# Clustered attention and its feed-forward: x split in PSUM and turned by one transposing DMA per pair of heads, and three PSUM banks handed out by a stored list

## The chip, the cores and the metric

One Trainium2 chip, one core of it. The metric is the time of one execution on the device in microseconds (us), lower is better; the time given is the median of several runs.

## The reference

```python
def _attn_ref(q, k, v, centroids):            # 4 x 8 x 768 x 64, 16 centroids of each head
    ...                                       # q_assign, k_assign: nearest centroid by cosine
    mask = q_assign[:, :, :, None] == k_assign[:, :, None, :]
    scores = scale * np.matmul(q, k.transpose(0, 1, 3, 2))
    scores = np.where(mask, scores, -1000000000.0)
    ...                                       # softmax over the keys
    return np.matmul(attn, v).astype(np.float32)

def _moe_ref(x, w_in, w_out):                 # 3072 x 512, 512 x 2048, 2048 x 512
    h = x @ w_in
    g = np.where(h >= 1, h, np.where(h <= -1, 0.0, (h + 1) ** 2 / 4.0))
    return (g @ w_out).astype(np.float32)
```

The attention's output, with the eight heads side by side, is the x of the second function.

## The kernel before

The work is cut into 12 units: a unit is one batch (of 4) and 256 of its 768 queries. A unit has four pairs of heads. For each pair, `at_scores` multiplies q by k on TensorE four times (two heads, two blocks of 128 queries), `soften` and `at_soft` take the exponential on VectorE and ScalarE and split it into two float16 parts (ScalarE the high part, GpSimd the low one, tile `hl` or `word`), and a transposing DMA on SyncE's queue (SP) turns both parts into `pT`, a ring of three buffers. `at_av` (L1178) multiplies `pT` by v into half of PSUM bank `banka`.

What `at_av` then does for units 1 to 11 is what the change touches. VectorE multiplies the result by the reciprocal row sums into the SBUF tile `rb` (`xn`, L1194 to L1199). TensorE turns `rb` back into the same place of `banka` in two float32 transpositions against the identity `idf` (L1202 to L1207). ScalarE copies it to float16, `x` high, and VectorE subtracts for `x` low (L1208 to L1210). That happens 44 times: 11 units of four pairs. Unit 0 has a path of its own (`at_av_first`) that is left alone.

`ffn1` (L1341) multiplies the weights by a unit's x, all four pairs in one accumulation, 24 matmuls of 256 columns for each of 8 blocks of the hidden layer; `ffn2` (L1373) multiplies the result `g` by the second weights into `pair` bank 83. Both run some units behind the attention, mixed into it. The weights are read, rounded and split on VectorE and ScalarE during the first units.

PSUM: two double banks `pair`, `banka`, and three banks `bankh`, `banki`, `bankj` that a `Ring` (L459) hands out in turn to `ffn1`, to the labels of the clusters and to small sums.

The order of the instructions is set by a planner. Every operation is recorded as a node with a price (L129); `Recorder.issue` (L349) simulates the engines forward and backward `BASE` times, moves the priorities by 141 stored seeds (`NUDGES`, L50), simulates once more, and each engine gets its instructions in that order. An engine works strictly in its order, SP too: a DMA that waits for its data holds up all DMAs behind it.

Of the kernel before, what the change touches and what calls it, by code (L numbers as in the profile page):

```python
# [10 lines left out]
F16 = mybir.dt.float16  # L11
BF16 = mybir.dt.bfloat16
F32 = mybir.dt.float32
U32 = mybir.dt.uint32
AF = mybir.ActivationFunctionType
ALU = mybir.AluOpType
# [29 lines left out]
TURN, TURN_WAIT = dict(vector=185, gpsimd=118), 200  # L46

LOOK, MARGIN = 0.4, 4000
BASE = 11
NUDGES = (  # L50
# [16 lines left out]
)  # L67


# [11 lines left out]
class Recorder:  # L81
# [9 lines left out]
    def __init__(self, tc):  # L91
        self.tc, self.nc = tc, tc.nc
        self.leads = []
        self.nodes, self.seen, self.open, self.step, self.ev = [], {}, None, -99, 0
        for name in ("tensor", "scalar", "vector", "gpsimd", "sync"):
            setattr(self, name, Engine(self, name, getattr(tc.nc, name)))
# [362 lines left out]
class Ring:  # L459


    def __init__(self, bufs):
        self.bufs, self.i = bufs, -1

    def extend(self, buf):

        n = (self.i + 1) % len(self.bufs)
        self.bufs, self.i = [buf] + self.bufs[n:] + self.bufs[:n], -1

    def __call__(self, *shape, dtype):  # L470
        self.i += 1
        return view(self.bufs[self.i % len(self.bufs)], shape, dtype)


def view(buf, shape, dtype):
    n = 1
    for k in shape:
        n *= k
    ap = buf.bitcast(dtype)[:, :n]
    if len(shape) > 1:  # L480
        names = "abcd"[: len(shape)]
        ap = ap.rearrange(
            "p (" + " ".join(names) + ") -> p " + " ".join(names), **dict(zip(names[1:], shape[1:]))
        )
    return ap
# [3 lines left out]
def tile_clustered_attention_moe(  # L489
# [11 lines left out]
    B, H, S, D = q.shape  # L501
# [5 lines left out]
    P = 128  # L507
    T = S // P
    NP = H // 2
    CT = 2  # L510
    NCH = T // CT
    CQ = CT * P
# [16 lines left out]
    rec = Recorder(tc)  # L529
    const = ctx.enter_context(tc.tile_pool(name="const", bufs=1))  # L530
    psum = ctx.enter_context(tc.tile_pool(name="psum", bufs=1, space=PSUM))
    rings = {}

    def tiles(name, n, size):
        return [const.tile([P, size // 4], U32, name=f"{name}{i}") for i in range(n)]

    def new(tag, shape, dtype, n=1):

        if tag not in rings:
            size = mybir.dt.size(dtype)  # L540
            for k in shape:
                size *= k
            rings[tag] = Ring(tiles(tag, n, -(-size // 32) * 32))
        return rings[tag](*shape, dtype=dtype)


    slots = tiles("kv", NP, 3 * 3072)

    qs = tiles("q", 2, 8192)
    rings["qn"] = Ring(tiles("qn", 1, 4096))  # L550
    rings["o"] = Ring(tiles("o", 1, 4096))
    rings["vb"] = rings["o"]

# [4 lines left out]
    halves = wk[1:] + blocks[:-1]  # L558
    rings["w32"] = Ring(wk[:1])
    rings["x"] = Ring(tiles("x", 3, 4096))  # L560
    rings["g"] = Ring(tiles("g", 2, 2048))

    nb = tiles("n", 1, 2 * 3072)[0]
    nats = [nb[:, :768], nb[:, 768:]]
    x1, x2 = rings["x"].bufs[1:3]
    k_one = [view(x[:, i * 384 : (i + 1) * 384], [T, 2, D], BF16) for x in (x2, x1) for i in range(2)]
    rings["hl"] = Ring(tiles("hl", 3, 3072))
    rings["koT"] = Ring([x[:, i * 384 : (i + 1) * 384] for x in (rings["o"].bufs[0], rings["hl"].bufs[2]) for i in range(2)])
    q_one, q_oneT = (view(x[:, :512], [NP * CT, P], BF16) for x in rings["hl"].bufs[:2])
    q_one = q_one.rearrange("p n (j c) -> p n j c", j=2)  # L570
# [4 lines left out]

    pair = [psum.tile([P, 1024], F32, name=f"pair{i}") for i in range(2)]
    bank_a, *one = [psum.tile([P, 512], F32, name=f"bank{x}") for x in "ahij"]
    hid = Ring(one)
    av = Ring([bank_a[:, :CQ], bank_a[:, CQ:]])
    start = cycle([0, 1]).__next__  # L580

    def early():
# [595 lines left out]
    def at_av(b, hp, c):  # L1178
        u = b * NCH + c
        if u == 0:  # L1180
            return at_av_first(hp)
        e, kv = A.pop((b, hp, c)), KV[b, hp]
        pv = px = av(CQ, dtype=F32)
        for t in range(CT):
            with rec.group():
                for j in range(2):
                    to = pv[:, (t * 2 + j) * D : (t * 2 + j + 1) * D]
                    for kc in range(T):
                        for i, (va, pa) in enumerate(((0, 0), (1, 0), (0, 1))):
                            rec.tensor.matmul(  # L1190
                                to, e["pT", t][:, pa * T + kc, j], kv["vs"][:, va, j, kc * D : (kc + 1) * D],
                                start=(kc == i == 0), stop=(kc == T - 1 and i == 2),
                            )
        xn = new("rb", [CT * 2, D], F32)  # L1194
        rr = e["rs"].rearrange("p (j t) -> p t j", j=2).unsqueeze(3).to_broadcast([P, CT, 2, D])
        rec.vector.tensor_tensor(
            out=xn.rearrange("p (t j) d -> p t j d", j=2), in0=pv.rearrange("p (t j d) -> p t j d", t=CT, j=2),
            in1=rr, op=ALU.mult,
        )  # L1199
        if hp == 0:  # L1200
            X[u] = new("x", [2, NP, CQ], F16)
        with rec.group():  # L1202
            for t in range(CT):
                rec.tensor.matmul(
                    px[:, t * P : (t + 1) * P], xn[:, 2 * t : 2 * t + 2].rearrange("p j d -> p (j d)"), idf,
                    start=True, stop=True, is_transpose=True,
                )  # L1207
        hi, lo = X[u][:, 0, hp], X[u][:, 1, hp]  # L1208
        rec.scalar.copy(hi, px)
        rec.vector.tensor_tensor(out=lo, in0=px, in1=hi, op=ALU.subtract)  # L1210

    X = {}

# [127 lines left out]
    def ffn1(u, f):  # L1341
        if u == 0:
            return ffn1_first(f)
        if u == 2 and f == 0:
            more = dict(r=wk[0][:, :512], g=wk[0][:, 512:], sS=word[:, :768], hl=word[:, 768:1536], qn=blocks[-1])
            for name, buf in more.items():
                rings[name].extend(buf)
        e = FS[u, f]
        x = X[u]
        ph = hid(2, CQ, dtype=F32)  # L1350
        for s in range(2):
            with rec.group():
                for hp in range(NP):
                    for i, (wa, xa) in enumerate(((0, 0), (0, 1), (1, 0))):
                        rec.tensor.matmul(
                            ph[:, s],
                            w1[f][:, wa, hp, s * P : (s + 1) * P],
                            x[:, xa, hp],
                            start=(hp == 0 and i == 0),
                            stop=(hp == NP - 1 and i == 2),  # L1360
                        )
        phf = ph.rearrange("p s q -> p (s q)")

        r = new("hl" if u == NU - 1 else "r", [2 * CQ], F32, 1)
        rec.vector.tensor_scalar(out=r, in0=phf, scalar1=e["lo"], scalar2=e["hi"], op0=ALU.max, op1=ALU.min)
        rec.scalar.activation(out=r, in_=r, func=AF.Square, bias=e["ra"], scale=e["rs"])
        rec.vector.scalar_tensor_tensor(out=r, in0=phf, scalar=e["gs"], in1=r, op0=ALU.mult, op1=ALU.max)
        g = new("g", [2, 2 * CQ], F16)
        rec.scalar.copy(g[:, 0], r)
        rec.gpsimd.tensor_tensor(out=g[:, 1], in0=r, in1=g[:, 0], op=ALU.subtract)  # L1370
        F[u, f] = g
# [184 lines left out]
```

## Time and profile before

| | |
|---|---|
| median of 3 runs | 839.02 us (838.34 to 839.78) |
| the profiled execution | 836.59 us |
| its span, first to last instruction | 834.8 us |
| TensorE busy | 819.3 us, 98% |
| VectorE, ScalarE, GpSimd busy | 631.6, 646.8, 485.1 us |
| DMA queue of SP, share of 16 engines | 83.5% |

The profiled execution lies 2.4 us below the median of the runs, and 1.8 us of it lie outside the span. A busy TensorE counts the modelled end of each matmul, so the true cost of an instruction is read from start to start. All instructions pass through one helper, so every row carries the line L363, and groups are told apart by tile names.

### The profile page before, as it was taken

How to read it: one execution, taken by the hardware profiler on the slowest of the kernel's cores; microseconds unless marked ns; L12 is line 12 of the kernel's file. 1: busy time of each engine (PE TensorE's matmuls, PEld its weight loads, DVE VectorE, ACT ScalarE, POOL GpSimd, SP SyncE). 2: the span in 40 equal slices, each digit the busy share in tenths (PEclk: the TensorE clock that was granted, in tenths of full speed). 3: DMA queues.
4: the chain of work that ended last, by engine and by line, in shares of the span. 5: the costliest groups of instructions: out<-in, count | busy, mean ns of one | idle time of the engine just before them, and what ended most of it. 6: DMA issues, size and time to landing. Idle time of an engine off the chain costs nothing.

```text
span 834.8 us, 21762 instructions
## 1 busy us (share of the span) xinstructions
PE 819.3 (98%) x8495; PEld 586.2 (70%) x8495; DVE 631.6 (76%) x1430; ACT 646.8 (77%) x1168; POOL 485.1 (58%) x541
## 2 busy tenths in 40 slices
PE   9998999999999999999999999999999999999998
PEld 7655767667667676777677677677767777676776
DVE  4999999999997767578888767579987776554322
ACT  5999976889878788787788788788887697766322
POOL 2004756568767667656767676656666666665121
PEclk9999999999999999999999999999999999999999
DMA  9869999998999979999999988999999869665100
GB/s 332 271 169 165 179 225 226 224 181 158 206 181 163 195 167 182 174 184 175 173 197 164 198 171 157 178 192 199 178 185 162 163 137 162 106 130 95 20 26 26
DMA packets 405415, 141.44 MB, mean 169 GB/s; under 512 B 373952, under 2 KB 397504, under 8 KB 405312
## 3 DMA queue, kind: packets, MB, share of 16 engines
q1 hardware_dynamic: 405312, 140.05, 83.5%
q8 instruction: 66, 1.08, 0.5%
q14 instruction: 37, 0.30, 0.1%
HBM read 40.40 MB, written 6.29 MB: 56 GB/s over the span
## 4 chain that ended last, share of the span: by engine, by line
PE 76%; DVE 14%; DMA 4%; issue 3%; ACT 2%; POOL 1%; SPq 0%; DVEq 0%; POOLq 0%
PE pair L363 37%; PE banka L363 11%; PE banki L363 10%; PE bankh L363 9%; PE bankj L363 9%; DVE sS L363 4%; DVE w L363 3%; DMA q<-in_q_dram 1%; DMA w<-in_moe_w_out_dram 1%; DVE r L363 1%; DVE n L363 1%; DVE wk L363 1%; POOL hl L363 1%; DMA pT<-hl 1%; DMA kv<-n 1%
## 5 line engine op out<-in xcount | busy, mean ns | idle before, releaser
L363 POOL TENSOR_TENSOR hl<-sS,hl 128x384 f16<-128x384 f32 x212 | 210.0, 1011 | 96.1 <-ACT hl L363 70.1
L363 PE MATMUL pair<-w,g 128*128 128x512 f16 (+2 forms) x796 | 202.6, 393 | 0.0
L363 PEld LDWEIGHTS <-w 128*128 128x128 f16 x1848 | 178.0, 98 | 30.5 <-issue 1.3
L363 DVE CUSTOM_DVE_ANT_0 sS<-pair,zero,er 128x768 f32<-128x768 f32 x157 | 158.8, 1012 | 48.2 <-PE pair L363 39.5
L363 ACT ACTIVATE sS<-sS,sbi 128x768 f32<-128x768 f32 x157 | 146.5, 933 | 53.9 <-DVE sbi L363 50.0
L363 PE MATMUL pair<-kv,q 128*128 128x384 f16 (+1 forms) x768 | 158.3, 341 | 2.1 <-DVE sbi L363 1.9
L363 PEld LDWEIGHTS <-g 128*128 128x128 f16 x762 | 73.0, 98 | 68.6
L363 PEld LDWEIGHTS <-pT 128*128 128x128 f16 x3168 | 103.0, 98 | 9.4 <-issue 0.6
L363 PEld LDWEIGHTS <-q 128*128 128x128 f16 x880 | 71.6, 97 | 48.3 <-issue 8.0
L363 PE MATMUL banka<-kv,pT 128*128 128x64 f16 x3168 | 105.4, 193 | 0.0
L363 ACT CAST hl<-sS 128x768 f16<-128x768 f32 x106 | 87.4, 825 | 1.7 <-DMA pT<-hl 0.7
L363 PE MATMUL banki<-x,w 128*128 128x256 f16 (+1 forms) x672 | 86.0, 280 | 0.0
L363 PE MATMUL bankh<-x,w 128*128 128x256 f16 (+1 forms) x672 | 85.8, 280 | 0.1
L363 PEld LDWEIGHTS <-wk 128*128 128x128 f16 x606 | 58.0, 98 | 34.8 <-issue 0.6
L363 POOL TENSOR_TENSOR hl<-word,hl 128x384 f16<-128x384 f32 x70 | 63.1, 921 | 31.3 <-ACT hl L363 20.4
L363 PE MATMUL bankj<-x,w 128*128 128x256 f16 (+1 forms) x632 | 80.5, 278 | 0.3 <-DVE r L363 0.3
L363 POOL TENSOR_TENSOR word<-sS,word 128x384 f16<-128x384 f32 x70 | 64.0, 932 | 24.8 <-ACT word L363 22.6
L363 PE MATMUL pair<-w,wk 128*128 128x512 f16 x324 | 76.3, 373 | 0.0
L363 POOL TENSOR_TENSOR g<-r,g 128x512 f16<-128x512 f32 x32 | 39.8, 1244 | 26.1 <-ACT g L363 26.1
L363 ACT ACTIVATE word<-word,sbi 128x768 f32<-128x768 f32 x35 | 32.7, 935 | 20.3 <-DVE sbi L363 19.8
L363 DVE CUSTOM_DVE_ANT_0 word<-pair,zero,er 128x768 f32<-128x768 f32 x35 | 35.5, 1015 | 13.5 <-PE pair L363 12.8
L363 ACT ACTIVATE r<-r,f_ra,f_rs 128x512 f32<-128x512 f32 x44 | 35.6, 809 | 13.0 <-DVE r L363 12.9
(294 smaller groups left out, 1319.3 us busy)
## 6 DMA issues: line engine op xcount, KB each, us to landing
w<-in_moe_w_out_dram SPq DMA_DIRECT2D x14, 512.0 KB, 4.4
kv<-in_k_dram SPq DMA_DIRECT2D x16, 384.0 KB, 4.5
q<-in_q_dram SPq DMA_DIRECT2D x12, 512.0 KB, 5.3
kv<-in_v_dram SPq DMA_DIRECT2D x16, 384.0 KB, 4.0
out_dram<-o SPq DMA_DIRECT2D x11, 512.0 KB, 3.8
w<-in_moe_w_in_dram SPq DMA_DIRECT2D x10, 512.0 KB, 7.8
word<-in_moe_w_in_dram SPq DMA_DIRECT2D x6, 512.0 KB, 5.5
o<-in_v_dram SPq DMA_DIRECT2D x8, 384.0 KB, 4.0
```

Source lines behind the costliest of these rows:

```text
L363: fn(*args, **kw)
```

## The change

The product is scaled in place in PSUM by VectorE. ScalarE then copies it to float16 into the first half of a `rb` of the same size (1 KB a partition), VectorE writes the remainder into the second half, and one transposing DMA on SP turns the four blocks of 128x128 (high and low of the two query blocks) into `x`, which is now laid out by pair, then high and low. The TensorE transpositions are gone. A `Ring` can take its places from a stored string; `bankh`, `banki`, `bankj` are handed out by such a string of 214 digits, the other rings go on in turn. `BASE` is 2 instead of 11, and the seeds are 129 other ones.

```diff
-BASE = 11
+PICKS = {'hid': '0000101220110012000122112212112101202201120212020110...'}
+BASE = 2
...
     def __call__(self, *shape, dtype):
-        self.i += 1
-        return view(self.bufs[self.i % len(self.bufs)], shape, dtype)
+        self.i = int(next(self.picks, (self.i + 1) % len(self.bufs)))
+        return view(self.bufs[self.i], shape, dtype)
...
-    hid = Ring(one)
+    hid = Ring(one, "hid")
...
-        xn = new("rb", [CT * 2, D], F32)
         rr = e["rs"].rearrange("p (j t) -> p t j", j=2).unsqueeze(3).to_broadcast([P, CT, 2, D])
-        rec.vector.tensor_tensor(
-            out=xn.rearrange("p (t j) d -> p t j d", j=2), in0=pv.rearrange("p (t j d) -> p t j d", t=CT, j=2),
-            in1=rr, op=ALU.mult,
-        )
+        pf = pv.rearrange("p (t j d) -> p t j d", t=CT, j=2)
+        rec.vector.tensor_tensor(out=pf, in0=pf, in1=rr, op=ALU.mult)
+        xn = new("rb", [2, CQ], F16)
+        rec.scalar.copy(xn[:, 0], pv)
+        rec.vector.tensor_tensor(out=xn[:, 1], in0=pv, in1=xn[:, 0], op=ALU.subtract)
         if hp == 0:
-            X[u] = new("x", [2, NP, CQ], F16)
-        with rec.group():
-            for t in range(CT):
-                rec.tensor.matmul(
-                    px[:, t * P : (t + 1) * P], xn[:, 2 * t : 2 * t + 2].rearrange("p j d -> p (j d)"), idf,
-                    start=True, stop=True, is_transpose=True,
-                )
-        hi, lo = X[u][:, 0, hp], X[u][:, 1, hp]
-        rec.scalar.copy(hi, px)
-        rec.vector.tensor_tensor(out=lo, in0=px, in1=hi, op=ALU.subtract)
+            X[u] = new("x", [NP, 2, CQ], F16)
+        rec.sync.dma_start_transpose(
+            out=X[u][:, hp].rearrange("p a (t q) -> p (a t) q", q=P), in_=xn.rearrange("p a f -> p (a f)")
+        )
...
-                            x[:, xa, hp],
+                            x[:, hp, xa],
```

The order of every engine changes with the seeds. Two places matter below. The first is SP's end: `pT` is the turned exponential, `rb` the split product, `x_75` the x of unit 11. Before:

```order
L363 DMA_TRANSPOSE pT_146<-hl_81 128x12x128
L363 DMA out_dram<-o_68 128x1024
L363 DMA_TRANSPOSE pT_147<-hl_79 128x12x128
L363 DMA_TRANSPOSE pT_147<-hl_80 128x12x128
L363 DMA_TRANSPOSE pT_145<-word_71 128x12x128
L363 DMA_TRANSPOSE pT_145<-hl_81 128x12x128
L363 DMA_TRANSPOSE pT_146<-hl_79 128x12x128
L363 DMA_TRANSPOSE pT_146<-hl_80 128x12x128
L363 DMA_TRANSPOSE pT_147<-word_71 128x12x128
L363 DMA_TRANSPOSE pT_147<-hl_81 128x12x128
L363 DMA out_dram<-o_68 128x1024
L363 DMA out_dram<-o_68 128x512 x2
```

And with the change:

```order
L363 DMA_TRANSPOSE pT_147<-hl_80 128x12x128
L363 DMA_TRANSPOSE pT_145<-hl_81 128x12x128
L363 DMA_TRANSPOSE x_75<-rb_159 128x4x128
L363 DMA_TRANSPOSE pT_145<-word_71 128x12x128
L363 DMA_TRANSPOSE pT_146<-hl_79 128x12x128
L363 DMA_TRANSPOSE pT_146<-hl_80 128x12x128
L363 DMA_TRANSPOSE pT_147<-hl_81 128x12x128
L363 DMA_TRANSPOSE x_75<-rb_159 128x4x128
L363 DMA_TRANSPOSE pT_147<-word_71 128x12x128
L363 DMA_TRANSPOSE x_75<-rb_159 128x4x128
L363 DMA out_dram<-o_68 128x1024
L363 DMA out_dram<-o_68 128x512 x2
```

One transposition of x stands among every four of `pT`, with others behind it, and the last one stands after the last `pT`.

The second place is TensorE from the last product with v (`banka<-kv_64`) to the first use of unit 11's x. Before, with the first row of each run of equal ones:

```order
L363 MATMUL banka<-kv_64,pT_147 128x64
...
L363 MATMUL banki<-x_74,w_72 128x256
...
L363 MATMUL pair_83<-w_72,wk_69 128x512
...
L363 MATMUL banka<-idf,rb_159 128x128 x2
...
L363 MATMUL banki<-x_74,w_72 128x256
...
L363 MATMUL pair_83<-w_72,g_76 128x512
...
L363 MATMUL bankj<-x_75,wk_70 128x256
```

And with the change:

```order
L363 MATMUL banka<-kv_64,pT_147 128x64
...
L363 MATMUL pair_83<-w_72,wk_69 128x512
...
L363 MATMUL bankh<-x_74,w_72 128x256
...
L363 MATMUL pair_83<-w_72,g_76 128x512
...
L363 MATMUL banki<-x_75,wk_70 128x256
```

The runs between them are 12 of 256 columns, 12 of 512, the transpositions, 12 of 256 and 12 of 512 before, and 6 of 512, 12 of 256 and 12 of 512 now.

## Rows read from the trace of the kernel before

**Rows 1.** The page: busy time of each engine, the granted clock of TensorE in 40 slices, and the chain that ended last, by engine.
```profile
PE 819.3 (98%) x8495; PEld 586.2 (70%) x8495; DVE 631.6 (76%) x1430; ACT 646.8 (77%) x1168; POOL 485.1 (58%) x541
PEclk9999999999999999999999999999999999999999
PE 76%; DVE 14%; DMA 4%; issue 3%; ACT 2%; POOL 1%; SPq 0%; DVEq 0%; POOLq 0%
```

**Rows 2.** Busy time of each engine by stretch: start and end of the stretch, its length, then busy us (instructions) of PE, PEld, DVE, ACT and POOL, the granted clock, the DMA share and GB/s.
```profile
0.00:160.00 160.00, 149.12 (x1302) 105.77 (x1303) 146.17 (x309) 134.49 (x245) 63.69 (x93) 1.00 0.90 224
160.00:782.00 622.00, 621.18 (x6819) 443.81 (x6819) 470.07 (x1100) 496.85 (x901) 411.06 (x440) 1.00 0.89 168
782.00:835.00 53.00, 48.96 (x377) 36.64 (x374) 15.31 (x21) 15.47 (x23) 10.39 (x9) 1.00 0.06 21
...
0.00:40.00 40.00, 36.73 (x350) 27.96 (x351) 27.50 (x73) 30.23 (x51) 6.21 (x35) 1.00 0.88 304
40.00:100.00 60.00, 54.09 (x475) 37.82 (x474) 59.38 (x135) 57.76 (x117) 23.34 (x27) 1.00 0.81 169
100.00:160.00 60.00, 58.30 (x484) 40.00 (x481) 59.29 (x106) 46.50 (x79) 34.13 (x32) 1.00 1.00 226
160.00:220.00 60.00, 59.86 (x625) 40.96 (x625) 58.09 (x137) 54.16 (x94) 41.45 (x38) 1.00 0.90 183
400.00:460.00 60.00, 59.75 (x673) 42.59 (x672) 51.64 (x131) 50.19 (x90) 42.66 (x48) 1.00 0.99 174
```

**Rows 3.** Waits of TensorE from 160 us to the end (its matmuls, then its weight loads), in full but for two groups of issue: engine, what it was about to do, what it waited for, us in total, times, longest.
```profile
PE bankj L363 <- DVE r L363: 0.3, 1, 0.3
PE bankj L363 <- DMA kv<-n: 0.3, 1, 0.3
...
PEld L363 <- DMA kv<-n: 0.6, 2, 0.4
PEld L363 <- DVE n L363: 0.6, 1, 0.6
PEld banka L363 <- DVE rb L363: 0.5, 2, 0.3
```

**Rows 4.** The same for its matmuls in the first 160 us, two rows of nine.
```profile
PE banki L363 <- ACT pT L363: 1.6, 3, 0.7
PE bankj L363 <- ACT pT L363: 1.5, 3, 1.0
```

**Rows 5.** The timeline around one end of a pair: start, us, engine, what.
```profile
408.05 0.81 PE L363 MATMUL pair<-kv,q 128*128 128x384 f16 x4
408.19 0.42 DVE L363 TENSOR_TENSOR rb<-banka,rs 128x256 f32<-128x256 f32 x1
...
408.70 0.40 PE L363 MATMUL banka<-idf,rb 128*128 128x128 f32 x2
...
408.94 1.47 PE L363 MATMUL bankj<-x,w 128*128 128x256 f16 x12
```

**Rows 6.** Groups of equal instructions over the whole span: busy us, mean ns of one, idle before.
```profile
L363 DVE TENSOR_TENSOR rb<-banka,rs 128x256 f32<-128x256 f32 x44 | 18.5, 420 | 11.8 <-PE banka L363 11.4 <-PE bankj L363 0.2
L363 DVE TENSOR_TENSOR x<-banka,x 128x256 f16<-128x256 f32 x44 | 18.2, 416 | 9.3 <-ACT x L363 9.2
L363 PE MATMUL banka<-idf,rb 128*128 128x128 f32 x88 | 17.1, 276 | 1.0 <-DVE w_am L363 1.0
L363 ACT CAST x<-banka 128x256 f16<-128x256 f32 x44 | 15.8, 361 | 7.5 <-PE banka L363 7.3
L363 DVE TENSOR_TENSOR bankj<-bankj,mx 128x256 f32<-128x256 f32 x6 | 2.6, 428 | 0.1
```

**Rows 7.** Busy time of the instructions that touch `rb` alone, by stretch, columns as in rows 2 without POOL.
```profile
100.00:160.00 60.00, 1.58 (x8) 0.96 (x8) 1.64 (x4) 0.00 (x0) 1.00 1.00 226
160.00:220.00 60.00, 1.18 (x6) 0.77 (x6) 1.25 (x3) 0.00 (x0) 1.00 0.90 183
```

**Rows 8.** SP's issue of the one transposition of four 128x128 blocks (`q` of one pair) that starts at 407.0 us, with the ns for which it held SP and its time from issue to landing, then the longest wait of SP over the whole span.
```profile
L363 SPq DMA_TRANSPOSE q<-w x1: 1189/1189/1189, 407.0 to 407.0; - x1
DMA to landing us min/median/max: 2.4/2.4/2.4
...
SPq L363 <- POOL hl L363: 130.8, 76, 4.1
```

**Rows 9.** All transposing DMAs of `pT<-hl` and `q<-w`: count, median us to landing.
```profile
pT<-hl SPq DMA_TRANSPOSE x141, 4.1
q<-w SPq DMA_TRANSPOSE x11, 4.4
```

**Rows 10.** The end of the attention, from the chain that ended last (start, us, what) and from the timeline.
```profile
776.45 2.10 PE banka L363 x72
778.55 1.31 PE banki L363 x12
779.86 2.59 PE pair L363 x12
...
778.92 0.41 DVE L363 TENSOR_TENSOR rb<-banka,rs 128x256 f32<-128x256 f32 x1
...
782.28 0.38 PE L363 MATMUL banka<-idf,rb 128*128 128x128 f32 x2
...
782.50 1.47 PE L363 MATMUL banki<-x,w 128*128 128x256 f16 x12
782.70 0.37 ACT L363 CAST x<-banka 128x256 f16<-128x256 f32 x1 [2.97 <-PE banka L363]
783.11 0.42 DVE L363 TENSOR_TENSOR x<-banka,x 128x256 f16<-128x256 f32 x1 [3.77 <-ACT x L363]
```

More of the change, by code (lines that the diff above doesn't have):

```diff
@@ L48 @@
 LOOK, MARGIN = 0.4, 4000
-BASE = 11
+PICKS = {'hid': '0000101220110012000122112212112101202201120212020110210021201101200022110220010012100112202211210120112022200201100221221010011222001101122120210001211111122111202001212211000221121100002012221011111111111010101010'}
+BASE = 2
 NUDGES = (
[16 rows of a table removed]
[15 rows of a table added]
 )
@@ L459, with __init__ @@
 class Ring:
-    def __init__(self, bufs):
-        self.bufs, self.i = bufs, -1
+    def __init__(self, bufs, name=None):
+        self.bufs, self.i, self.picks = bufs, -1, iter(PICKS.get(name, ""))
     def extend(self, buf):
-        n = (self.i + 1) % len(self.bufs)
-        self.bufs, self.i = [buf] + self.bufs[n:] + self.bufs[:n], -1
+        self.bufs = self.bufs + [buf]
     def __call__(self, *shape, dtype):
-        self.i += 1
-        return view(self.bufs[self.i % len(self.bufs)], shape, dtype)
+        self.i = int(next(self.picks, (self.i + 1) % len(self.bufs)))
+        return view(self.bufs[self.i], shape, dtype)
 def view(buf, shape, dtype):
@@ L542, in new @@
                 size *= k
-            rings[tag] = Ring(tiles(tag, n, -(-size // 32) * 32))
+            rings[tag] = Ring(tiles(tag, n, -(-size // 32) * 32), tag)
         return rings[tag](*shape, dtype=dtype)
@@ L549, in tile_clustered_attention_moe @@
     qs = tiles("q", 2, 8192)
-    rings["qn"] = Ring(tiles("qn", 1, 4096))
+    rings["qn"] = Ring(tiles("qn", 1, 4096), "qn")
     rings["o"] = Ring(tiles("o", 1, 4096))
@@ L560, in tile_clustered_attention_moe @@
     rings["x"] = Ring(tiles("x", 3, 4096))
-    rings["g"] = Ring(tiles("g", 2, 2048))
+    rings["g"] = Ring(tiles("g", 2, 2048), "g")
     nb = tiles("n", 1, 2 * 3072)[0]
@@ L566, in tile_clustered_attention_moe @@
     k_one = [view(x[:, i * 384 : (i + 1) * 384], [T, 2, D], BF16) for x in (x2, x1) for i in range(2)]
-    rings["hl"] = Ring(tiles("hl", 3, 3072))
+    rings["hl"] = Ring(tiles("hl", 3, 3072), "hl")
     rings["koT"] = Ring([x[:, i * 384 : (i + 1) * 384] for x in (rings["o"].bufs[0], rings["hl"].bufs[2]) for i in range(2)])
@@ L577, in tile_clustered_attention_moe @@
     bank_a, *one = [psum.tile([P, 512], F32, name=f"bank{x}") for x in "ahij"]
-    hid = Ring(one)
-    av = Ring([bank_a[:, :CQ], bank_a[:, CQ:]])
+    hid = Ring(one, "hid")
+    av = Ring([bank_a[:, :CQ], bank_a[:, CQ:]], "av")
     start = cycle([0, 1]).__next__
@@ L1193, in at_av @@
                             )
-        xn = new("rb", [CT * 2, D], F32)
         rr = e["rs"].rearrange("p (j t) -> p t j", j=2).unsqueeze(3).to_broadcast([P, CT, 2, D])
-        rec.vector.tensor_tensor(
-            out=xn.rearrange("p (t j) d -> p t j d", j=2), in0=pv.rearrange("p (t j d) -> p t j d", t=CT, j=2),
-            in1=rr, op=ALU.mult,
-        )
-        if hp == 0:
-            X[u] = new("x", [2, NP, CQ], F16)
-        with rec.group():
-            for t in range(CT):
-                rec.tensor.matmul(
-                    px[:, t * P : (t + 1) * P], xn[:, 2 * t : 2 * t + 2].rearrange("p j d -> p (j d)"), idf,
-                    start=True, stop=True, is_transpose=True,
-                )
-        hi, lo = X[u][:, 0, hp], X[u][:, 1, hp]
-        rec.scalar.copy(hi, px)
-        rec.vector.tensor_tensor(out=lo, in0=px, in1=hi, op=ALU.subtract)
+        pf = pv.rearrange("p (t j d) -> p t j d", t=CT, j=2)
[3 more added lines that the diff above has]
+        rec.vector.tensor_tensor(out=xn[:, 1], in0=pv, in1=xn[:, 0], op=ALU.subtract)
+        if hp == 0:
+            X[u] = new("x", [NP, 2, CQ], F16)
+        rec.sync.dma_start_transpose(
+            out=X[u][:, hp].rearrange("p a (t q) -> p (a t) q", q=P), in_=xn.rearrange("p a f -> p (a f)")
+        )
     X = {}
```

31 rows, old and new, of the table NUDGES are left out of this document.

## The prediction

> **What bounds the kernel now.** I read the page first. TensorE is busy for 98% of the span at the full granted clock from the first slice to the last, and 76% of the chain that ended last is TensorE, 14% VectorE and 4% DMA [rows 1]. So what counts is how many columns TensorE has to stream, if nothing else stops it. The table by stretch says where that holds. From 160 to 782 us TensorE is busy for 621.18 of 622 us [rows 2], and its waits from there to the end add up to 0.6 us for matmuls and 1.7 us for weight loads that a releaser is named for [rows 3]. There TensorE is the bound in the strict sense: take a matmul out, and all that follows moves up by its streaming time. Before 160 us it isn't: TensorE is idle for 160 - 149.1 = 10.9 us, and VectorE is busy for 59.38 and 59.29 of 60 us in the stretches from 40 to 160, and still for 58.09 in the next one [rows 2]; the rounding and splitting of the weights sits there. After 782 us there is only the feed-forward of the last unit, with the DMA queue idle (0.06).
>
> The second full resource is the DMA queue: 0.89 of 16 engines from 160 to 782 us, 0.99 in single stretches [rows 2]. The change takes from the first resource and gives to the second. That is the question here.
>
> **The change part by part.**
>
> *The TensorE transpositions go.* The group says 88 instructions, 17.1 us busy [rows 6], but that counts modelled ends. From start to start a pair of them costs 408.94 - 408.70 = 0.24 us in the middle and 782.50 - 782.28 = 0.22 us at the end [rows 5, 10]. I take 0.23: 44 x 0.23 = 10.1 us off TensorE; the bounds are 44 x 0.22 = 9.7 and the group's 17.1. The wait for `rb` that goes with them is 0.5 us in all [rows 3], and I leave it out.
>
> *Some of it lies where TensorE isn't alone.* Four pairs (8 instructions) fall between 100 and 160 us and three between 160 and 220 us [rows 7], where VectorE is full and loses no work. Those seven are worth 7 x 0.23 = 1.6 us. TensorE is all but full there too (58.30 and 59.86 of 60), and what it doesn't do there it must do later, so I count half of it as lost: +0.8 us, bounds 0 and 1.6.
>
> *VectorE and ScalarE.* The number of operations is the same. The product now goes to PSUM instead of SBUF: 428 ns is what a VectorE operation of that size takes from PSUM to PSUM, against 420 [rows 6], so 44 x 0.008 = 0.4 us spread over an engine with 24% idle. The copy and the subtraction keep their shapes and only write `rb` instead of `x` (361 and 416 ns [rows 6]). Nothing; the cover is VectorE's idle time after 220 us, and without it the 0.4 us would show. `banka` comes free sooner, since no transposition stands between the product and the copy.
>
> *The 44 transposing DMAs.* The nearest row is a transposition of the same four blocks that starts at 407.0 us: it holds SP for 1.19 us and lands after 2.4 us [rows 8]. One moves 128 x 512 x 2 bytes = 0.131 MB. In the stretch from 400 to 460 us, where transpositions are most of the traffic, a share of 0.99 moved 174 GB/s [rows 2], so such a DMA takes 0.131 MB / 174 GB/s = 0.75 us of the 16 engines. Bounds: 0.38 us at the 304 GB/s x (1 / 0.88) of the first 40 us, and the whole 2.4 us if nothing else ran beside it. About 40 of them lie in the 622 us stretch, which becomes some 10 us shorter. The queue's load there is then 0.89 x 622 + 40 x 0.75 = 554 + 30 = 584 us of 612, a share of 0.95. It fits. SP itself spends its longest waits for GpSimd's data, 130.8 us [rows 8], so it has the 44 x 1.19 = 52 us to spare. I put the DMAs at nothing in the middle. The cover is that TensorE doesn't wait for a single `pT` after 160 us [rows 3], and that x is needed some units later. If the cover fails, it is the `pT` behind an x transposition in SP's order that comes late, and the product with v waits for it. The Trainium skill's page "Advanced Engine Details and Errata", section "X-Bar Transpose (TRN2)", has it that such transfers are as fast as plain ones, at 350 to 400 GB/s. An estimate from that page's 375 GB/s is 0.35 us each, 14 us instead of 30 on the queue; the forecast would be the same and the queue rival below less likely, but the 174 GB/s of the full stretch speak against it.
>
> *The last unit.* There x has no units of slack. From the end of the last product with v to x the trace gives, for the new chain: 0.37 us to VectorE's start (778.55 to 778.92), 0.41, then 0.04 + 0.37 for ScalarE, 0.04 + 0.42 for VectorE [rows 10], 0.1 to SP, and 2.4 to land [rows 8]: 4.2 us. The new order puts 6 matmuls of 512, 12 of 256 and 12 of 512 columns in between, by the rows 1.3 + 1.31 + 2.59 = 5.2 us [rows 10]. One microsecond to spare; with the 4.4 us that is the median landing of its group [rows 9] TensorE would stand for 1.0 us, and one feed-forward operation ahead on VectorE adds 0.8. I take +0.5, bounds 0 and 2.
>
> *The banks and the new order.* TensorE's waits for ScalarE to empty `banki` and `bankj` into `pT` are 1.6 + 1.5 = 3.1 us of the first 160 us [rows 4]. Handing banks out by a list can avoid some of them, and only there, since later there are no waits to avoid. I take -1.0; bounds -3.1, and +3 for a start that another order makes worse by as much.
>
> **The sum:** -10.1 + 0.8 + 0.5 - 1.0 = -9.8 us. The profiled execution goes from 836.6 to 826.8 us. The median of the runs shown is 2.4 us above it, so 839.0 becomes 829.2 us, 1.2% faster. Its own range, by the bounds: 824.5 to 833.
>
> **The rivals.**
>
> *Half is given back.* The pipeline stays full but some `pT` or `kv` land late now and then: in the trace of before one wait for such a DMA does show, 0.3 us and 0.6 us [rows 3]. If every second pair of heads costs TensorE 0.23 us, 22 x 0.23 = 5 us come back: 834 us. For it: the DMA share of 0.95. Against it: TensorE has feed-forward matmuls of older units to be put between, in the new order as in the old.
>
> *The DMA queue becomes the bound (slower).* The price that decides is how long one added transposition keeps the others out. There are 612 - 554 = 58 us free in the stretch for 40 of them: up to 1.45 us each nothing is lost, above 1.45 + 10 / 40 = 1.7 us the kernel gets slower. If a transposition shuts the queue for nearly its whole 2.4 us, say 2.0, the stretch takes 554 + 80 = 634 us instead of 612, and the kernel 829 + 22 = 851 us. For it: the queue at 0.99 in places, 2.4 us from issue to landing [rows 2, 8]. Against it: a landing is mostly latency, and the transpositions three times as large land in 4.1 us [rows 9], which is (4.1 - 2.4) / 2 = 0.85 us for each further 0.131 MB. The Trainium skill's page "VectorE: DVE Perf Modes", sections "The three transpose paths" and "Rules for kernel authors", prefers TensorE where PSUM is an acceptable destination, and gives 390 ns for a 128x128 block on TensorE and 1309 ns by DMA. By that page an estimate for four blocks one after the other is 5.2 us, far above the deciding price; the 2.4 us of the same shape contradicts it, and so does TensorE's 0.12 us a block.
>
> *No change.* The early stretch, bound by VectorE, or a worse start eats all of it: 10.1 us would have to come from the first 220 us or from the tail's 2 us, where the largest single term is 3 us. Time 838 to 840.
>
> **How the numbers follow.** The forecast has 0.67, half given back 0.18, no change 0.05, the DMA queue 0.10. What a measurement of this kernel can tell from no change is about 0.2%, 1.7 us. Faster by more than that: 0.67 + 0.18 = 0.85; within it 0.05; slower 0.10. The range takes the forecast's lower bound and reaches up over the second case: 824.5 to 836.5, which leaves out the last two cases and a little of the ends.
>
> **What the changed profile would show.** TensorE's matmuls fall by 88 and `banka<-idf,rb` is gone; TensorE's busy share in the middle stays above 99%, and its waits after 160 us stay under 3 us. SP has 44 more DMA_TRANSPOSE rows `x<-rb`, landing in 2.4 to 5 us, and the DMA share between 160 us and the end of the attention rises to about 0.95. The last product with v ends about 9 us earlier. It is wrong if TensorE waits for `pT` in the middle (the queue), if the stretch up to 220 us is longer than before by more than 2 us (VectorE or the order), or if TensorE stands for more than 2 us before the first matmul on unit 11's x.

## The result and the profile after

The changed kernel takes 844.5 us (median of 4 runs, 842.98 to 845.28) beside 839.04 us (838.34 to 839.78) for the kernel before: 1.0068 times as long, 95% interval 1.0053 to 1.0084. It is slower by 0.7%, where 1.2% faster was forecast. The profiled execution took 842.98 us, its span is 841.2 us, 6.4 more than before.

The page's busy times, clock and chain, which answer to [rows 1]:

```profile
PE 814.3 (97%) x8407; PEld 574.6 (68%) x8407; DVE 634.5 (75%) x1430; ACT 647.6 (77%) x1168; POOL 487.9 (58%) x541
PEclk9998999999999999999999999999999999999999
PE 59%; DVE 6%; DMA 4%; ACT 2%; issue 2%; POOL 1%; SPq 0%; DVEq 0%; ACTq 0%; POOLq 0%
```

The 88 transpositions are gone, and TensorE is busy for 5.0 us less (819.3 to 814.3). But it is idle for 841.2 - 814.3 = 26.9 us, where it was 834.8 - 819.3 = 15.5: 11.4 more. 11.4 - 5.0 is the 6.4 us. The chain names no new engine. Its shares can't be set beside those of before: it can be followed back only to 212 us, and they add up to 74%, of which TensorE has 59 (before, 76 of 100).

Where the idle time lies is in the table by stretch (columns as in [rows 2]):

```profile
0.00:40.00 40.00, 36.51 (x367) 27.56 (x368) 27.71 (x74) 31.21 (x53) 6.80 (x34) 1.00 0.81 278
40.00:100.00 60.00, 52.96 (x420) 35.63 (x418) 57.26 (x129) 57.41 (x114) 19.69 (x26) 0.94 0.86 196
100.00:160.00 60.00, 58.46 (x497) 39.04 (x496) 59.12 (x100) 45.28 (x77) 39.71 (x33) 1.00 1.00 217
160.00:220.00 60.00, 57.76 (x581) 39.38 (x580) 57.79 (x134) 52.91 (x89) 38.66 (x37) 1.00 0.93 188
160.00:782.00 622.00, 610.91 (x6678) 430.85 (x6677) 473.11 (x1105) 496.73 (x902) 409.68 (x441) 1.00 0.96 177
```

Up to 160 us TensorE is busy for 147.93 us (149.12 before): 1.2 us lost. From 160 to 782 us it is idle for 11.1 us, where it was 0.8 [rows 2]: here are ten of the eleven microseconds, in the stretch that was bound by TensorE alone. The DMA share is 0.96.

What TensorE waited for from 160 us to the end, matmuls, in full (columns as in [rows 3], where two waits of 0.3 us stood):

```profile
PE pair L363 <- DVE sbi L363: 3.0, 8, 0.7
PE banka L363 <- DMA pT<-hl: 1.2, 1, 1.2
PE banka L363 <- DMA pT<-word: 1.0, 1, 1.0
PE banki L363 <- DVE er L363: 0.9, 1, 0.9
PE bankj L363 <- DVE wk L363: 0.8, 1, 0.8
PE banki L363 <- DVE r L363: 0.8, 1, 0.8
PE bankh L363 <- DVE zs L363: 0.7, 1, 0.7
PE bankj L363 <- DVE aq L363: 0.6, 1, 0.6
PE bankj L363 <- DVE n L363: 0.5, 1, 0.5
PE pair L363 <- DVE w L363: 0.5, 1, 0.5
PE bankh L363 <- DVE has L363: 0.4, 1, 0.4
PE bankh L363 <- DMA x<-rb: 0.3, 1, 0.3
PE pair L363 <- ACT o L363: 0.2, 1, 0.2
```

The sum is 10.9 us, 8.2 of it ended by VectorE, 2.2 by a `pT` and 0.3 by the new x. Two of the waits are where a `pT` is late. Of those that VectorE ends, 6.6 us are for PSUM banks that it hasn't given back (`sbi`, `er`, `wk`, `r`, `zs`, `has`) and 1.6 us for data that it hasn't written yet (`aq`, `n`, `w`). One of the first kind in the timeline (start, us, engine, what), where the clusters' labels are worked out:

```profile
432.15 0.18 DVE L363 TENSOR_SCALAR has<-bankh 128x32 f32<-128x32 f32 x1
...
432.38 1.47 PE L363 MATMUL bankh<-x,w 128*128 128x256 f16 x12 [0.36 <-DVE has L363]
432.44 0.85 DVE L363 TENSOR_TENSOR banki<-zs,has 128x64 f32<-128x64 f32 x1
...
433.40 1.01 DVE L363 CUSTOM_DVE_ANT_0 sS<-pair,zero,er 128x768 f32<-128x768 f32 x1
...
434.59 0.16 DVE L363 TENSOR_TENSOR er<-banki,zm 128x4 f32<-128x4 f32 x1
...
434.80 1.36 PE L363 MATMUL banki<-x,w 128*128 128x256 f16 x11 [0.95 <-DVE er L363]
```

VectorE works without a pause, an instruction of 1.01 us for the attention stands ahead of the 0.16 us that free the bank, and TensorE's next matmuls want that bank. Neither x nor its DMA has a part in it: what counts is which instruction stands where.

The groups that the operation consists of (as in [rows 6]), and the landings (as in [rows 9]; `x<-rb` is new):

```profile
L363 DVE TENSOR_TENSOR banka<-banka,rs 128x256 f32<-128x256 f32 x44 | 18.7, 426 | 15.2 <-PE banka L363 15.1
L363 DVE TENSOR_TENSOR rb<-banka,rb 128x256 f16<-128x256 f32 x44 | 18.3, 417 | 5.9 <-ACT rb L363 5.9
L363 ACT CAST rb<-banka 128x256 f16<-128x256 f32 x44 | 15.9, 362 | 7.1 <-DVE banka L363 5.7 <-DVE ik L363 1.2
```

```profile
pT<-hl SPq DMA_TRANSPOSE x141, 4.2
x<-rb SPq DMA_TRANSPOSE x44, 2.8
q<-w SPq DMA_TRANSPOSE x11, 5.0
```

A `pT<-hl` lands 0.1 us and a `q<-w` 0.6 us later than before, in a queue with 44 more transfers. And the end of the attention, which answers to [rows 10]:

```profile
786.69 1.21 PE L363 MATMUL banka<-kv,pT 128*128 128x64 f16 x36
...
787.94 0.43 DVE L363 TENSOR_TENSOR banka<-banka,rs 128x256 f32<-128x256 f32 x1 [1.14 <-PE banka L363]
788.41 0.37 ACT L363 CAST rb<-banka 128x256 f16<-128x256 f32 x1 [0.88 <-DVE banka L363]
788.81 0.42 DVE L363 TENSOR_TENSOR rb<-banka,rb 128x256 f16<-128x256 f32 x1 [0.44 <-ACT rb L363]
...
789.26 1.19 SPq L363 DMA_TRANSPOSE x<-rb  x1
...
792.93 2.24 PE L363 MATMUL banki<-x,wk 128*128 128x256 f16 x19
```

The last product with v ends at 787.9 us, 9.3 later than before. TensorE doesn't stop between that and the first matmul on unit 11's x.

### The profile page after: what moved, and what is told of

The parts are those of the page before. It is cut to its first block, busy times and chain, and to the rows that moved or that the text cites. A ratio compares the mean times of both kernels' runs of the same rounds, so it can differ in the third digit from the quotient of the medians.

```text
span 841.2 us, 21715 instructions
## 1 busy us (share of the span) xinstructions
PE 814.3 (97%) x8407; PEld 574.6 (68%) x8407; DVE 634.5 (75%) x1430; ACT 647.6 (77%) x1168; POOL 487.9 (58%) x541
## 3 DMA queue, kind: packets, MB, share of 16 engines
q1 hardware_dynamic: 429248, 145.83, 88.1%
## 4 chain that ended last, share of the span: by engine, by line
PE 59%; DVE 6%; DMA 4%; ACT 2%; issue 2%; POOL 1%; SPq 0%; DVEq 0%; ACTq 0%; POOLq 0%
PE pair L363 30%; PE banki L363 12%; PE banka L363 8%; PE bankj L363 5%; PE bankh L363 4%; DVE sS L363 1%; DMA pT<-hl 1%; DMA pT<-word 1%; DVE wk L363 1%; DMA q<-in_q_dram 1%; ACT hl L363 1%; POOL hl L363 1%; DMA o<-in_v_dram 1%; DVE r L363 1%; DVE bankh L363 1%
## 5 line engine op out<-in xcount | busy, mean ns | idle before, releaser
L363 POOL TENSOR_TENSOR hl<-sS,hl 128x384 f16<-128x384 f32 x214 | 214.6, 1025 | 91.5 <-ACT hl L363 72.1
L363 PE MATMUL banki<-x,w 128*128 128x256 f16 (+1 forms) x1064 | 131.3, 276 | 0.9 <-DVE er L363 0.9
L363 PE MATMUL banka<-kv,pT 128*128 128x64 f16 x3168 | 107.3, 193 | 2.4 <-DMA pT<-hl 1.2
L363 PEld LDWEIGHTS <-q 128*128 128x128 f16 x880 | 71.3, 97 | 55.8 <-issue 13.7
L363 PE MATMUL bankj<-x,w 128*128 128x256 f16 (+1 forms) x504 | 66.0, 283 | 0.9 <-DVE wk L363 0.8
L363 PE MATMUL bankh<-x,w 128*128 128x256 f16 (+1 forms) x408 | 54.7, 285 | 1.1 <-DVE zs L363 0.7
L363 DVE CUSTOM_DVE_ANT_0 word<-pair,zero,er 128x768 f32<-128x768 f32 x34 | 34.5, 1014 | 10.4 <-PE pair L363 7.1
L363 POOL TENSOR_TENSOR g<-wk,g 128x512 f16<-128x512 f32 x24 | 28.4, 1181 | 22.8 <-ACT g L363 22.6
```

Of the source, the lines that this page charges most:

```text
L363: fn(*args, **kw)
```

## The experiments

Each ran beside the kernel before on one and the same chip (the runs are from several chips); the ratio is to that, and 0.001 is 0.84 us. The third column is TensorE's idle time from 160 to 780 us in the profile (the expectations count its waits in nearly the same stretch). "Operation" is x by DMA, without the list. "Plan" is what the planner sees; "seeds" without "before's" are others that were found for that planner.

| run | ratio (95%) | idle, us |
|---|---|---|
| before | 1 | 0.8 |
| the change | 1.0068 (1.0053 to 1.0084) | 11.1 |
| its order, DMAs left out | 1.0071 (1.0047 to 1.0095) | 9.0 |
| before's order, 40 DMAs more, outside of the plan | 1.0056 (1.0041 to 1.0071) | 3.7 |
| before's order, x by DMA for units 1 to 10 | 1.0132 (1.0099 to 1.0166) | 14.6 |
| before, no seeds | 1.0049 (1.0034 to 1.0064) | 2.7 |
| operation, before's seeds | 1.0203 (1.0186 to 1.0220) | 16.6 |
| operation, no seeds | 1.0188 (1.0161 to 1.0215) | 18.0 |
| operation without its DMAs, no seeds | 1.0011 (0.9997 to 1.0024) | 8.5 |
| operation, added DMAs priced at a hundredth, no seeds | 1.0012 (1.0002 to 1.0022) | 9.6 |
| before, no seeds, 40 DMAs in the plan | 1.0237 (1.0221 to 1.0253) | 16.7 |
| operation, a hundredth, 38 seeds | 1.0037 (1.0025 to 1.0049) | 14.0 |
| operation, half price, 40 seeds | 1.0005 (0.9988 to 1.0021) | 6.7 |
| operation, all turning DMAs at 4.7, seeds | 1.0081 (1.0056 to 1.0106) | 13.9 |
| before, all turning DMAs at 4.7, seeds | 1.0109 (1.0088 to 1.0131) | 12.5 |
| operation, all at 4.0, seeds | 1.0201 (1.0178 to 1.0224) | 19.0 |
| before, list, no seeds | 1.0044 (1.0032 to 1.0056) | 2.3 |
| operation, list, no seeds | 1.0191 (1.0167 to 1.0214) | 17.9 |
| before, VectorE relieved, no seeds | 0.9996 (0.9985 to 1.0006) | 3.1 |
| operation without DMAs, VectorE relieved, no seeds | 0.9941 (0.9922 to 0.9960) | 5.1 |

### Is it the transfers?

The order of the change, with the 44 DMAs taken out after planning (x is written straight, so it stays untransposed). `n_hi` and `n_lo` are the nodes of the copy and of the subtraction, the last node is the DMA:

```diff
+        xd = X[u][:, hp]
+        n_hi.calls = [(nc.scalar.copy, (xd[:, 0], pv), {})]
+        n_lo.calls = [(nc.vector.tensor_tensor, (), dict(out=xd[:, 1], in0=pv, in1=xd[:, 0], op=ALU.subtract))]
+        rec.nodes[-1].calls = []
```

> The changed kernel with every instruction in the order it has there, but the 44 transposing DMAs of x are left out: ScalarE and VectorE write the two halves straight into x, which so holds the untransposed values. Theory Q (the DMA queue: the added transfers make pT and q land late, and TensorE waits): TensorE's idle time between 160 and 700 us falls from about 13 us to under 4, and the time to 831 to 836 us. Theory P (the plan: the new order and bank list stall by themselves, the DMAs are nearly free): 842 to 845 us with the same stalls.

Measured 1.0071, the change's own ratio with an interval of 2 us either way, and TensorE still stands for 9.0 us: theory P. The transfers aren't what costs the change most of its time; its order is.

The other way round, the order of before and 40 such DMAs put behind `x` low, from an older x into the free `rb`:

```diff
+        if u > 1:
+          rec.nodes[-1].calls.append((nc.sync.dma_start_transpose, (), dict(
+            out=xn.rearrange("p t d -> p (t d)").bitcast(F16).rearrange("p (t q) -> p t q", q=P),
+            in_=X[u - 1][:, 1, :2].rearrange("p n q -> p (n q)"),
+        )))
```

> The kernel before in its old order, TensorE transpositions included, with 40 transposing DMAs of the same size added (units 2 to 11, an older unit's x into the rb that is free by then): the price of the DMAs alone. Theory L: 837 to 839 us, nothing. Theory Q: 842 to 852 us.

1.0056: 4.7 us, where theory L expected nothing. The idle time grows by 2.9 us. A busy TensorE hides a part of what is lost, so it is counted once more from each matmul's start to the next, less the median of its shape in the kernel before (its streaming time). By that count TensorE lost 4.3 us more after 160 us than before, 0.11 us for each DMA. It also lost 1.8 us more in the first 160 us, where none of the 40 DMAs runs yet and the mean clock is 0.98, against 1.00 in the profile of before. So in an order that has no room for them the transfers do cost something, but far less than the 2 us each of the queue rival.

And x turned by DMA at the places where TensorE turned it, in the order of before:

```diff
+        if u < NU - 1:
+            xh = xn.rearrange("p t d -> p (t d)").bitcast(F16)
+            to = X[u][:, hp].rearrange("p a (t q) -> p (a t) q", q=P)
+            n_mul.calls = [(nc.vector.tensor_tensor, (), dict(out=pf, in0=pf, in1=rr, op=ALU.mult))]
+            n_pe.calls = []
+            n_hi.calls = [(nc.scalar.copy, (xh[:, :CQ], pv), {})]
+            n_lo.calls = [
+                (nc.vector.tensor_tensor, (), dict(out=xh[:, CQ:], in0=pv, in1=xh[:, :CQ], op=ALU.subtract)),
+                (nc.sync.dma_start_transpose, (), dict(out=to, in_=xh)),
+            ]
```

> The kernel before, every engine in its old order, with its seeds and rings; only for units 1 to 10 the two TensorE transpositions of each pair are dropped, the product stays in PSUM, the split goes to rb and one transposing DMA stands on SP where VectorE's subtraction stood in the order of time (40 DMAs; unit 11 keeps TensorE). Theory L: the saving shows, 40 x 0.23 = 9 us less, 828 to 831 us. Theory Q: 836 to 850 us, TensorE waits for pT.

1.0132, with 6.5 us of waits for `x<-rb` in three places where a matmul on the new x came too early, 2.1 us for `q` and 1.6 us for `pT`. In this order the saving isn't to be had: the operation does need one of its own.

### Is it the order, and what in it?

The operation alone under the seeds and rings of before, then both kernels without seeds:

```diff
-NUDGES = (
...
+NUDGES = ()
```

> The split in PSUM and the transposing DMA alone: the seeds, BASE = 11 and the rotating rings are those of the kernel before (the order still comes out anew, since the planner sees other operations). Theory Q: stalls on landings as in the changed kernel, 840 to 850 us. Theory P: the saving shows, 829 to 834 us.

> The kernel before with an empty list of seeds: the planner's own order, not one picked out of many. It is the base for the next run. Both theories: slower than 839 us, by how much tells what the picked seeds are worth; 842 to 860 us.

> The split in PSUM and the transposing DMA with an empty list of seeds, BASE = 11 and rotating rings: against the kernel before without seeds it prices the operation alone, with neither side picked. Theory Q: the same as that kernel or up to 10 us slower. Theory P: 7 to 11 us faster than it.

1.0203, 1.0049 and 1.0188: 854.4, 841.6 and 853.9 us, the first and the last slower than either theory expected. The seeds are worth 4.1 us to the kernel before. Without seeds on either side the operation loses 0.0139, or 11.7 us.

Next, what in the plan does that: once the DMAs left out of it (x untransposed again), once left in but priced at next to nothing:

```diff
-            return 33, kb, "transpose" in op
+            return 33, kb * (0.01 if kb == 128 and 'transpose' in op and out.shape[1] == 4 and len(self.nodes) and node_is_x(out) else 1), "transpose" in op
```

> The run with the operation alone and no seeds, but x is written straight by ScalarE and VectorE, untransposed, and no DMA of x is in the plan at all. It prices what the DMAs cost through the plan. Theory L (the loss is made by the plan, which leaves gaps for transfers that it believes late) and theory Q (the DMA queue is really too full): both 829 to 836 us, 8 to 12 us under the unseeded kernel before (841.6 us). If it stays near 853.9 us both are wrong and the split in PSUM itself is slow.

> The operation alone without seeds, all 44 DMAs there, but the planner prices their transfer at a hundredth: an order that does not make room for them on the queue. Theory L: 832 to 842 us. Theory Q: 850 us and more, with TensorE waiting for pT over 10 us in all.

1.0011 and 1.0012 (the first, 838.9 us, is slower than both theories expected). The second program does the same work as the unseeded operation at 1.0188, all 44 DMAs on the chip; only a number in the planner differs, and it is 14.8 us faster. Beside the first, the DMAs cost nothing that shows. The planner has 5.6 ns per KB for a transposing transfer, so 128 x 5.6 = 717 ns for one of x, and puts all transfers in one line (`self.ring` in its simulation, with SP held back by `self.hw = max(self.hw, self.ring - 1000)`): 44 of them are 31.5 us more in a line that is nearly full.

The cleanest form of the question is the kernel before, TensorE's transpositions and all, with 40 DMAs that nothing needs, recorded where the run above had appended them behind the planner's back:

```diff
+        if u > 1:
+            rec.sync.dma_start_transpose(
+                out=xn.rearrange("p t d -> p (t d)").bitcast(F16).rearrange("p (t q) -> p t q", q=P),
+                in_=X[u - 1][:, 1, :2].rearrange("p n q -> p (n q)"),
+            )
```

> The kernel before without seeds, TensorE's transpositions kept, and 40 transposing DMAs of the size of x's from one SBUF tile to another, which nothing needs, now recorded as operations that the planner sees and prices. Beside 841.55 us without them and 842.87 us for the same DMAs outside of the plan, in the seeded order. Theory L (the planner, told of the DMAs, opens gaps for them): 850 to 856 us, TensorE's waits from 160 to 790 us 10 us or more. Theory D (the plan's gaps need the operation, in which x depends on the DMA): 841.5 to 846 us, waits 4 to 7 us.

1.0237 beside 1.0049 without them: 15.8 us, more than theory L expected, with not one instruction of the operation in it. The 40 DMAs also run on the chip here, and this order wasn't run without them; in the seeded order, outside of the plan, they cost 4.7 us. As far as that carries over, some 11 of the 15.8 us are the plan's. The trace names no wait that one of the 40 ended. TensorE's longest waits there are again for VectorE:

```profile
PE pair L346 <- DVE sbi L346: 6.1, 8, 1.1
PE pair L346 <- ACT o L346: 1.6, 2, 1.1
PE bankh L346 <- DVE r L346: 1.3, 1, 1.3
PE bankj L346 <- DMA q<-qn: 1.2, 1, 1.2
```

So VectorE's names in such rows are not a mark of the operation. The reading is that they end the waits of an order in which TensorE's other work has been put elsewhere; that wasn't followed instruction by instruction.

### Is the price wrong, and can the operation win?

The next five runs have seeds of their own: the operation with the added DMAs at a hundredth and at half of their price, with all transposing DMAs at 4.7 and at 4.0 ns per KB, and the kernel before at 4.7. The last three change two lines of the planner, of which one is shown:

```diff
-            self.ring = max(self.ring, self.hw + (650 if tr else 784)) + kb * (5.6 if tr else 3.25)
+            self.ring = max(self.ring, self.hw + (650 if tr else 784)) + kb * (4.7 if tr else 3.25)
```

> The changed operation without the list of banks, planned as in the run before whose planner priced the 44 transpositions of x at a hundredth of their transfer, and now with 38 seeds found for that planner (BASE 10). Theory L (the planner's price made the loss; with an order of its own the operation gains): unseeded it took 838.93 us, seeds were worth 841.55 - 837.6 = 4 us to the kernel before, so 835 us, 833 to 836.5, TensorE's waits between 160 and 780 us fall from 11.7 to 5 to 8 us, and none of them is for pT. Theory V (where k and v of the next batch are prepared VectorE is full, so whatever TensorE saves there comes back as waits for it): the waits stay at 10 to 12 us, 837 to 839.5 us. Theory Q (the DMA queue limits): waits for pT and x appear as TensorE gets denser, 840 us or more.

> The operation of the change without the list; the planner has the transfer of the 44 added DMAs at half its price and all others at the old one; 40 seeds found for that. Beside 838.93 us (a hundredth, no seeds) and 841.91 us (a hundredth, seeds). If a middle price lets the order use the operation: 833 to 836.5 us, waits from 160 to 790 us 4 to 8 us, few of them for DMAs. If VectorE at the batch changes and the queue at 0.96 take the saving back whatever the order: 837.5 to 842 us, waits 10 us or more.

> The operation of the change, its 44 DMAs included, no list; the planner prices every transposing DMA at 4.7 instead of 5.6 ns per KB, with 34 seeds found for that. Theory L (the price is what costs, and a mild correction of it lets the order use the operation): 832 to 836 us, TensorE's waits from 160 to 790 us 4 to 8 us. Theory V (the saving comes back as waits for VectorE where it is full, at any price): 837 to 840 us, waits 10 to 14 us that VectorE ends. Theory Q (the real queue is as slow as the planner has it, so a lower price makes transfers late): 840 to 845 us, with waits for q, pT and kv.

> The kernel before, with TensorE's transpositions, at the same price of 4.7 and 16 seeds found in the same search time. It stands beside the run of the operation at that price: Theory L: 836 to 839 us here, so the operation gains 3 us or more. Theory V: 836 to 839 here and within 1.5 us of the operation. Theory Q: 839 us or more, with waits for DMAs, since the old program has the same other transpositions.

> As the operation at 4.7, at 4.0 ns per KB, with 27 seeds found for that. Theory L: no worse than at 4.7, 832 to 836 us. Theory V: 837 to 840 us. Theory Q: worse than at 4.7 by 2 us or more, with more waits for q, pT and kv.

The best, the operation at half price, takes the time of the kernel before (1.0005); none is faster than that kernel. Price and seeds change together in these runs, and seeds that are better in the planner need not be so on the chip: at a hundredth the program with 38 seeds is slower (1.0037) than the one with none (1.0012). Its waits for matmuls are 13.7 us, of which VectorE ends 9.7 and a late `q` 3.2.

With all transposing DMAs at 4.7 the operation takes 1.0081, less than at 5.6 without seeds (1.0188) and not to be told from the change (1.0068); at 4.0 it takes 1.0201. The kernel before at 4.7 with 16 seeds (1.0109) is slower than at 5.6 with none (1.0049). TensorE's waits for matmuls from 160 us in that run, first rows:

```profile
PE bankh L346 <- DMA kv<-n: 3.0, 3, 2.5
PE pair L346 <- DMA q<-w: 2.3, 4, 0.9
PE bankj L346 <- DMA kv<-n: 2.3, 2, 1.3
```

So 5.6 is no mistake: the queue is nearly full, and an order that counts on a faster one waits for it. Nor is it one for the 44 transfers of x. The page's row of SP's queue (packets, MB, share of the span), with the change and with its order without the DMAs:

```profile
q1 hardware_dynamic: 429248, 145.83, 88.1%
q1 hardware_dynamic: 405312, 140.05, 84.8%
```

That is 88.1% of 841.2 us against 84.8% of 839.1 us, 29.5 us or 0.67 us for each; the prediction had 0.75 and the planner has 0.72. So the price fits what a transfer takes of the queue, and still the unseeded order that is made without it is 14.8 us faster. That this is because x has slack is likely (in the change TensorE's matmuls wait 0.3 us in all for the 44) but not shown.

### What holds the operation back when its DMAs are free?

Unseeded and without DMAs it gains 0.0038 (3.2 us) where TensorE streams 9.6 us less. Theory: VectorE, which is full until about 250 us. It was relieved in both kernels by zeros for the low halves of the weights:

```diff
-        split(w[:, 0], w[:, 1], tf, sw[:, n : n + 1])
+        rec.scalar.activation(out=w[:, 0], in_=tf, func=AF.Copy, scale=sw[:, n : n + 1])
+        rec.vector.tensor_scalar(out=w[:, 1], in0=w[:, 0], scalar1=0.0, scalar2=None, op0=ALU.mult)
```

> The kernel before without seeds, with VectorE relieved while it is full: the low halves of the weights are zeros, written by a 16-bit multiplication in the place of 16 subtractions of 1474 ns (the feed-forward's low terms are left out of the result, not out of TensorE's work). Theory V (VectorE is the second bound up to about 250 us): with some 18 us less on it the start gets denser, 836 to 840 us beside 841.55 without this. Theory N (only the order counts, VectorE doesn't): 840.5 to 842.5.

> The operation of the change without its DMAs and without seeds (x written straight and untransposed, 838.85 us when VectorE was not relieved), with the same relief of VectorE. What is read is the gain over the run beside it: unrelieved it was 841.55 - 838.85 = 2.7 us of 9.6 us that TensorE streams less. Theory V (VectorE, full up to about 250 us and at the batch changes, takes the rest back): the gain rises to 6 to 9 us, and TensorE's waits between 200 and 260 us, 5.2 us before, fall below 2. Theory N (the waits are those of a poorer order): the gain stays at 1 to 4 us and the waits stay.

Both get faster, by 4.4 and 5.9 us. In the profiles TensorE loses 2.5 and 4.7 us less before 160 us, from start to start, so VectorE does bound a part of the start. The operation's gain becomes 0.0055, 4.6 us. With intervals of 0.001 to 0.002 either way that is not told from 3.2, and it stays below the 6 us that the theory asked for. The other sign that it named is there: between 200 and 260 us TensorE is idle for 1.8 us, against 4.2 without the relief. Inconclusive.

### The list

```diff
-    hid = Ring(one)
+    hid = Ring(one, "hid")
```

> The kernel before with TensorE's transpositions, its three banks handed out by the change's list, no seeds: the list alone, beside the run of the kernel before without seeds (841.55 us, 1.0049). Theory A (the list is worth something by itself, as the -1.0 us of the prediction had it): 840.5 us, 838.5 to 841.5. Theory B (the list was fitted to the order of the change and fits no other): 844 us or more. Theory C (banks don't matter): 841 to 842.

> Operation and list of the change, the planner's price as it was (5.6), no seeds: beside 853.88 us of the same without the list. If the list alone is worth something to the operation: 846 to 850 us. If the seeds of the change win its 9.4 us and the list does nothing without them: 852 to 856 us. If the list was fitted to the seeds and fits no other order: over 856 us.

1.0044 beside 1.0049, and 1.0191 beside 1.0188: by itself the list is worth nothing to either kernel.

## Why the prediction was wrong

**The sum that was measured**, by ratios along a chain of runs: no seeds +4.1 us, the operation without DMAs -3.2, the DMAs on the chip but unpriced +0.1, their price in the plan +14.8, the list +0.2, the change's own seeds with `BASE` 2 -10.3. That is +5.7, the 0.0068. Each step has an uncertainty of 1 to 3 us, and taken in another order the steps would come out otherwise.

**The step that failed is the order.** The prediction gave "the banks and the new order" -1.0 us with bounds of -3.1 and +3, and held that a list could win something "only there", in the start, "since later there are no waits to avoid". That bounds a gain, not a loss. An order without waits can't be bettered, only kept or lost, and the new program is planned anew from its first instruction to its last. Counted from start to start, TensorE lost 14.2 us more after 160 us than before, and 9.0 of the 11.1 us of idle time are there without the DMAs too: the order by itself. So the other step, that after 160 us all that follows a matmul moves up when it is taken out, doesn't hold for a program whose order is made anew: without DMAs and seeds 3.2 of 9.6 us were won. The planner's price for a DMA stood in the code and was not weighed. Of the signs of being wrong that the prediction names, two came: a `pT` was waited for in the middle (2.2 us), and up to 220 us TensorE lost 4.8 us more.

**The DMAs "at nothing in the middle"** were right on the chip in the change's order, within the 2 us that the run without them can tell, and wrong in the sum. The queue's share of 0.95 was measured at 0.96, the landing forecast at 2.4 to 5 us had a median of 2.8, and `pT` lands 0.1 us later. (The Trainium skill's page "VectorE: DVE Perf Modes", section "The three transpose paths", gives 1309 ns for one block by DMA; the estimate of 5.2 us for four, one after the other, is not borne out by that median.) But the cover that was named, that TensorE waits for no `pT` [rows 3], belonged to an order that was planned without these DMAs.

**The transpositions** at 10.1 us: 88 x 109 ns = 9.6 us of streaming are gone, so the term's size stands.

**The early term** of +0.8, bounds 0 and 1.6, and the -1.0 of the banks belong together: before 160 us 1.9 us were lost from start to start, of which the clock (below) is a part. The waits for ScalarE's `pT`, in all banks, did fall there, from 3.8 to 2.2 us; all waits for matmuls rose from 10.4 to 11.9. How much of the 1.9 us belongs to which term isn't shown. From 160 to 220 us the 2.1 us more of idle time belong to the failed step.

**The last unit**, +0.5 with 4.2 us from the last product to x: the chain took 789.26 + 2.4 - 787.9 = 3.8 us with the landing of [rows 8], TensorE had other work until 792.93, and nothing was lost.

**The rivals.** The queue as the bound, 851 us, had the right sign, but its mechanism isn't there: waits for DMAs are 2.5 of 10.9 us, and of 11.1 us of idle time 9.0 stay when the DMAs go. "No change" named a worse start; most was lost in the middle. Half given back, 834 us, named late `pT`s, and there were two.

**The range**, 824.5 to 833 "by the bounds", isn't what its bounds add up to: that is 818.8 to 835.9 us. The 844.5 lies above either.

Open are two things: why an order that spares the queue leaves TensorE without other work at just these places, which wasn't followed in the planner, and how much of the 6 us between the streaming saved and the gain without DMAs is VectorE's.

## What to carry to other kernels

Where a planner makes the order, a new operation costs first what the planner believes of it: put it into the old program as an operation that nothing needs, and see what the order alone loses. Covers read from a trace hold for the order of that trace. If nothing waits in a long stretch, a new order can only add waits there, so its term reaches up by as much as the runs of other seeds differ, here 4 to 10 us, and a saving of 10 us need not outweigh it.

## What the runs showed of the hardware

TensorE's clock fell to its lower level, 1.2 GHz, in the start. In the change's profile (columns as in [rows 2]):

```profile
69.00:72.00 3.00, 1.52 (x16) 1.28 (x16) 2.14 (x8) 2.85 (x7) 2.33 (x4) 1.00 1.02 245
72.00:75.00 3.00, 1.29 (x12) 0.81 (x11) 1.95 (x4) 3.00 (x5) 0.00 (x0) 1.00 0.95 103
75.00:78.00 3.00, 1.82 (x14) 0.93 (x12) 3.00 (x7) 3.00 (x7) 1.60 (x2) 0.61 1.17 240
78.00:81.00 3.00, 3.00 (x20) 1.55 (x20) 3.00 (x7) 3.00 (x6) 0.79 (x2) 0.50 0.61 118
81.00:84.00 3.00, 3.00 (x21) 1.54 (x18) 2.96 (x6) 2.84 (x7) 2.06 (x3) 0.75 0.70 133
```

It had been busy for 1.52 and 1.29 of 3 us before it fell, and ran at half speed for (0.39 + 0.50 + 0.25) x 3 / 0.5 = 6.8 us, at most 3.4 us lost. It isn't the change's alone: other executions of the kernel before show a mean clock of 0.995 to 1.000, the changed one 0.994 to 0.996. It goes with a part of the scatter: the operation at a hundredth without seeds took 838.1 to 838.4 us in five runs, four of them at 0.996 and one at 0.994, and 839.5 to 840.4 in the other five, all at 0.993 or 0.994.

Forty more transposing DMAs of 128 KB, in the order of before, moved the queue's share between 160 and 780 us from 0.90 to 0.97 and the median landing of `pT` from 4.1 to 4.2 us. TensorE's waits for `kv`, `pT` and `q` after 160 us came to 2.7 us (0.3 before), and the kernel took 4.7 us longer.
